# Attention feeding a rational feed-forward: value products of half a query range in one run, with the small column-tiled products and the weight conversion placed next to it

## The chip, the cores and the metric

The kernel runs on one core of one Trainium2 chip. The metric is the device time of that core in microseconds (us). Three executions of the kernel before took 981.39, 981.89 and 984.1 us; the median is 981.89. The execution that was profiled took 982.12 us, of which 980.3 us lie between its first and its last instruction.

## The reference, cut to what matters

The first stage is attention in which a query sees only the keys of its own hash bucket; the second is a feed-forward layer with a rational function between its two products.

```python
# attention: q, k, v are (4, 8, 768, 64); proj is (64, 6)
q_bits = (einsum('bhsd,dk->bhsk', q, proj) > 0)          # the same for k
mask = q_bucket[:, :, :, None] == k_bucket[:, :, None, :]
scores = where(mask, scale * q @ k.T, -1e9)
scores = scores - max(scores, axis=-1)
attn = exp(scores)
attn = attn / (sum(attn, axis=-1) + 1e-9)
x = attn @ v                                             # (3072, 512) once the heads are side by side
# feed-forward: w_in (512, 2048), w_out (2048, 512)
h = x @ w_in
P = a0 + a1*h + a2*h**2 + a3*h**3
Q = 1 + |b0|*|h| + |b1|*h**2
out = (P / (Q + 1e-6)) @ w_out
```

## The kernel before, in words

**Attention.** The 32 heads are worked in 16 pairs (p = 0 to 15), two heads (h) on the two halves of the 128 partitions. A pair has twelve steps: two halves of the queries (hf, 384 each) by six tiles of keys (kt). Step s = 6 hf + kt makes the scores of one key tile against 384 queries, for both heads, transposed (keys on the partitions). Operands are split in a high and a low float32r part (q1, k1 and q2, k2), and the bucket mask and the row maximum are carried as additional rows of q1 and k1, so that one product of 77 rows and one of 128 rows give masked and shifted scores (`scores`, lines 246 to 262). Each goes to a PSUM bank of 512 columns, tag "s", of which there are three, and ScalarE takes the exponential into an SBUF tile E, of which there are six. GpSimd adds the E of three successive steps into an accumulator acc.

**Value products.** `values` (lines 264 to 271) multiplies a tile of v (64 columns for each head) with E and adds up over the six key tiles of a half in a PSUM bank of its own, tag "v". These matmuls use 64 columns of the array, one head on each half, while scores use all 128. The operands are plain float32, and each matmul stands in the profile as two. `values_out` brings the half to SBUF on ScalarE (col, then xo), `values_store` stores it.

**Other column-tiled products.** `sums` (lines 283 to 292) adds up the accumulators over the keys with a column of ones, in strips of 32 array columns (psu), and ScalarE copies the outcome (sr). `bits` (lines 188 to 201) projects q and k of two pairs on the hash vectors, also in strips of 32 (psb), and VectorE turns the signs into mask rows mb at its end; `penalties` scales them on ScalarE, `maskrows` moves them by four DMAs into q1 and k1.

**Row maxima.** `maxstep` (lines 215 to 223) makes one tile of scores for a pair that comes later, into one of two double banks (ps_a, psm; psb takes turns with it in the same two), and VectorE reduces it to a column of m. When all twelve are done, `shift_turn` transposes m on the array (pst), VectorE clamps it (mt), and `shift_rows` moves it by a DMA into row 76 of q1 of that pair. Its scores can only begin after that DMA has landed.

**Operands.** `high` casts q and k of pair p on ScalarE, `low` subtracts the cast on VectorE, `high_move`, `second_low` and `second_high` move halves by DMAs, `load` and `load_v` fetch the next raw ones.

**Weights.** `weights(i)`, 32 times, loads a 512 KB piece of w_in or w_out (stored as 64-bit floats), turns it into float32 by two ScalarE and three VectorE instructions, and splits it in a high part (ScalarE) and a low one (VectorE). Pieces of w_out are stored to DRAM again (wo_d).

**What sets the order.** All engines keep the order of the program. The program is written by a table: `at(p, s, f)` enters f under the time 12 p + s, and lines 447 to 449 call all entries in the order of their times, entries of one time in the order in which they were made. So one unit of that table is a step, and an engine's queue holds its instructions in that order: a ScalarE or VectorE instruction that waits holds up all that stand behind it, and SP, which issues nearly all DMAs, does so too.

**Feed-forward.** After pair 15, `Ffn.step` runs 128 times: a product with w_in (`Gemm1`, psh, from line 458, which uses the banks "s" and "v"), the rational function on ScalarE and VectorE, a product with w_out (pso).

## Time and profile before

| | |
|---|---|
| median of three runs | 981.89 us (981.39 to 984.1) |
| the profiled execution: device time | 982.12 us |
| its span, first to last instruction | 980.3 us |
| first product of the feed-forward | 437.2 us |
| TensorE matmul busy | 957.6 us, 98% |
| VectorE busy | 835.4 us, 85% |
| ScalarE busy | 679.2 us, 69% |
| GpSimd busy | 436.8 us, 45% |

All times in rows are counted from the start of the span. PE is TensorE's matmul stream, PEld its weight loads, DVE VectorE, ACT ScalarE, POOL GpSimd, SP the engine that issues DMAs. All instructions carry line 61, that of the helper which issues them, so rows are told apart by the tiles' names, output before the arrow: pss are scores, psm the products for the maxima, psv values, psu sums, psb bits, pst the turned maxima. A row of the chain gives the start, the length and the piece of work, as "149.70 1.45 PE psv L61 x8": eight matmul instructions in the trace, which are two steps of value products.

### The profile page before, as it was taken

Reading aid. Unit: us, or ns where it says so; the run is one execution under the profiler, and the core shown is the slowest. Engines: PE = TensorE matmul, PEld = TensorE weight load, DVE = VectorE, ACT = ScalarE, POOL = GpSimd, SP = SyncE. Lnnn points to the kernel's source line nnn. Section 1 sums busy time; section 2 is a strip of 40 time slices with the busy share of each in tenths; the row PEclk is TensorE's granted clock in tenths of the full one; section 3 lists DMA queues with packets and bytes.
Section 4 is the critical chain, followed back from the end, with each engine's and each line's share of the span. In section 5 each row is a group of like instructions: output and inputs, shape, how many; then the busy total and the mean of one; then the engine's idle time right before and its main releaser. Section 6 shows DMA issues by size and latency. Waiting matters only on the chain.

```text
span 980.3 us, 14803 instructions
## 1 busy us (share of the span) xinstructions
PE 957.6 (98%) x5009; PEld 744.8 (76%) x5009; DVE 835.4 (85%) x1200; ACT 679.2 (69%) x1411; POOL 436.8 (45%) x396
## 2 busy tenths in 40 slices
PE   5899999999999999999999999999999999999998
PEld 2556666666656666559999999999999999999996
DVE  5487778777877777568999999999999999999996
ACT  2356767676666666678777777777777777777775
POOL 1257776777677777782222222222222222222222
PEclk7699999999999999999999999999999999999999
DMA  7656676767686767737502111011011021110000
GB/s 202 175 169 185 184 201 171 202 186 198 183 254 211 242 190 206 236 126 260 169 1 66 33 49 48 1 65 33 1 65 33 1 65 33 62 36 1 33 1 32
DMA packets 50491, 112.97 MB, mean 115 GB/s; under 512 B 9296, under 2 KB 21968, under 8 KB 50416
## 3 DMA queue, kind: packets, MB, share of 16 engines
q1 hardware_dynamic: 49580, 110.59, 37.9%
q10 hardware_dynamic: 836, 1.44, 0.6%
q8 instruction: 39, 0.64, 0.3%
q14 instruction: 36, 0.29, 0.1%
HBM read 56.82 MB, written 21.17 MB: 80 GB/s over the span
## 4 chain that ended last, share of the span: by engine, by line
PE 92%; DVE 3%; DMA 3%; ACT 1%; SPq 0%; issue 0%; ACTq 0%; DVEq 0%
PE psh L61 27%; PE pso L61 27%; PE pss L61 15%; PE psv L61 13%; PE psm L61 6%; PE psu L61 2%; DVE m L61 1%; PE psb L61 1%; DMA wr<-w_out 1%; DMA q<-lo 0%; SPq L61 0%; DVE c L61 0%; DMA v<-v 0%; DMA prj<-proj 0%; DMA q<-mt 0%
## 5 line engine op out<-in xcount | busy, mean ns | idle before, releaser
L61 POOL TENSOR_TENSOR gl<-c,gh 128x384 fp32r<-128x384 f32 x128 | 140.4, 1097 | 395.4 <-ACT gh L61 368.8
L61 DVE TENSOR_REDUCE m<-psm 128x1 f32<-128x768 f32 x192 | 182.0, 952 | 92.5 <-PE psm L61 90.4
L61 PE MATMUL pso<-wo,gh 128*128 128x512 f32 x768 | 241.1, 395 | 0.0
L61 ACT ACTIVATE E<-pss 128x384 f32<-128x384 f32 x384 | 168.3, 492 | 79.7 <-PE pss L61 72.8
L61 POOL TENSOR_TENSOR acc<-E,E 128x384 f32<-128x384 f32 x128 | 150.9, 1199 | 113.9 <-ACT E L61 113.9
L61 PE MATMUL pss<-q,k 77*128 77x384 f32 (+1 forms) x768 | 180.2, 357 | 2.5 <-DMA q<-mt 1.5
L61 PEld LDWEIGHTS pss<-q,k 77*128 77x128 f32 (+1 forms) x768 | 134.0, 192 | 60.3 <-issue 50.1
L61 PE MATMUL psh<-xl,wi_hi 128*128 128x384 f32 x512 | 172.1, 336 | 0.0
L61 PE MATMUL psh<-xh,wi_hi 128*128 128x384 f32 x512 | 171.8, 336 | 0.0
L61 PE MATMUL psh<-xh,wi_lo 128*128 128x384 f32 x512 | 171.6, 335 | 0.0
L61 PEld LDWEIGHTS pso<-wo,gh 128*128 128x128 f32 x768 | 142.9, 188 | 23.7
L61 PE MATMUL pso<-wo,gl 128*128 128x512 f32 x384 | 152.3, 397 | 0.3 <-POOL gl L61 0.3
L61 ACT ACTIVATE h<-psh 128x384 f32<-128x384 f32 x128 | 62.9, 492 | 123.9 <-PE psh L61 123.9
L61 PE MATMUL psv<-E,v 128*64 128x385 f32 x768 | 148.3, 503 | 0.0
L61 DVE SCALAR_TENSOR_TENSOR c<-c,ab,r 128x384 f32<-128x384 f32 x128 | 146.9, 1147 | 0.0
L61 POOL TENSOR_TENSOR acc<-acc,E 128x384 f32<-128x384 f32 x128 | 142.7, 1135 | 7.8 <-ACT E L61 5.9
L61 PE MATMUL psm<-k,q 76*128 76x384 f32 x384 | 107.8, 365 | 7.0 <-DMA k<-mb 3.7
L61 PEld LDWEIGHTS psh<-xh,wi_hi 128*128 128x128 f32 x512 | 96.1, 188 | 6.3 <-ACT w L61 0.6
L61 PEld LDWEIGHTS psh<-xl,wi_hi 128*128 128x128 f32 x512 | 96.1, 188 | 5.1
L61 PEld LDWEIGHTS psh<-xh,wi_lo 128*128 128x128 f32 x512 | 96.2, 188 | 0.0
L61 PEld LDWEIGHTS psv<-E,v 128*64 128x64 f32 x768 | 45.7, 136 | 60.0 <-issue 52.4
L61 ACT ACTIVATE c<-psh,ab 128x384 f32<-128x384 f32 x128 | 86.5, 676 | 1.7 <-POOL gl L61 1.7
(62 smaller groups left out, 1233.8 us busy)
## 6 DMA issues: line engine op xcount, KB each, us to landing
q<-q SPq DMA_DIRECT2D x48, 192.0 KB
k<-k SPq DMA_DIRECT2D x48, 192.0 KB
wr<-w_in SPq DMA_DIRECT2D x16, 512.0 KB
wr<-w_out SPq DMA_DIRECT2D x16, 512.0 KB
wo_d<-wr SPq DMA_DIRECT2D x16, 512.0 KB
wo<-wo_d SPq DMA_DIRECT2D x16, 512.0 KB
q<-lo SPq DMA_DIRECT2D x32, 192.0 KB
k<-lo SPq DMA_DIRECT2D x32, 192.0 KB
```

What stands on the lines that cost most here:

```text
L61: return self.tc.keep_in_program_order(issue(*args, **kwargs))
```

## The change

1. **Values in one run.** The twelve matmuls of `values` for a whole half (six steps by two heads) now all stand at one place of the table, 12 p + 6.3 for the first half and 12 p + 12.3 for the second: right after the first step of the half that follows. Before, pairs 1 to 14 did them two steps at a time, pairs 0 and 15 one step at a time.
2. **Tiles.** A half's six E stay alive until that run, so there are seven E instead of six; acc goes from six to five. The bank "v" becomes a fourth bank "s", and values take turns with scores, sums and the turned maxima.
3. **Beside the run.** `sums` goes from 14.5 to 12.31, directly behind the run of the second half. `bits` is split: its matmuls go to 0.32 of every second pair, directly behind `sums`; the VectorE part becomes `bucket_rows` at 0.5. `high` goes from 0 and 1 to 0.4, `low` from 2 and 3 to 0.45, `penalties` from 3 to 1.2, `maskrows` of every second pair from 4 to 2.
4. **Weights beside it.** The two ScalarE conversions of a piece stand at 5.4 of each half, the three VectorE instructions at 6.25 and 6.26, the high part at 6.9, the low part at 9.4.
5. **Shift rows.** `shift_turn` goes from 8 to 6.9, `shift_rows` from 10 to 8, `load` from 6 to 6.5.

```diff
-ACCS = 6
+ACCS = 5
-    E = [ep.tile([P, 2, HQ + 2], F32, name=f"E{i}") for i in range(6)]
+    E = [ep.tile([P, 2, HQ + 2], F32, name=f"E{i}") for i in range(7)]
...
+        PSB[p + which[0]] = ps
+
+    def bucket_rows(p, which=(0, 1)):
+        sl = slice(64 * which[0], 64 * which[-1] + 64)
+        ps, mb = PSB.pop(p + which[0]), MB[p + which[0]][0]
         nc.vector.tensor_scalar(out=mb[sl], in0=ps[sl, :, 0:HQ], ...)
...
-            ps = ps_b.tile([P, 512], F32, tag="s", bufs=3, name=f"pss{p}_{s}_{h}")
+            ps = ps_b.tile([P, 512], F32, tag="s", bufs=4, name=f"pss{p}_{s}_{h}")
-            AV[p, hf] = ps_b.tile([P, 512], F32, tag="v", name=f"psv{p}_{hf}")
+            AV[p, hf] = ps_b.tile([P, 512], F32, tag="s", bufs=4, name=f"psv{p}_{hf}")
...
-            if not 0 < p < NPAIR - 1:
-                at(p, s + 2.3, values, p, s)
-            elif s % 2:
-                at(p, s + 1.3, values, p, s - 1)
-                at(p, s + 1.3, values, p, s)
-            if s % NT == NT - 1:
-                at(p, s + (1.3 if 0 < p < NPAIR - 1 else 2.3), values_out, p, s // NT)
+        for hf in range(2):
+            for i in range(NT):
+                at(p, 6 * hf + 6.3, values, p, 6 * hf + i)
+            at(p, 6 * hf + 6.3, values_out, p, hf)
...
-            at(p, 14.5, sums, p)
+            at(p, 12.31, sums, p)
...
             for t in range(2):
-                at(p - 2, t, high, p, t)
-                at(p - 2, 2 + t, low, p, t)
-            if p % 2 == 0:
-                at(p - 2, 3 if p == 2 else 2, bits, p)
-                at(p - 2, 4 if p == 2 else 3, penalties, p)
+                at(p - 2, t if first else 0.4, high, p, t)
+                at(p - 2, 2 + t if first else 0.45, low, p, t)
...
-            at(p - 1, 8 + d, shift_turn, p)
-            at(p - 1, 10 if d == 0 else 9.6, shift_rows, p)
+            at(p - 1, 9.5 if p == 1 else 6.9, shift_turn, p)
+            at(p - 1, 9.6 if p == 1 else 8, shift_rows, p)
...
-        o = 6 * i - 3
-        late = (10.5, 12.5, 13.5, 14.5) if i < 2 * NFC - 1 else (10.5, 10.8, 11, 11.2)
-        spread(0, [o + x for x in (4, 7, 8, 9) + late], weights(i))
+        times = (1, 5.4, 6.25, 6.26, 6.9, 9.4, 11) if i < 2 * NFC - 2 else (1, 4, 5, 6, 6.5, 7.5, 8)
+        if i == 2 * NFC - 1:
+            times = (0.5, 3, 3.5, 4, 4.5, 5.5, 6.2)
+        spread(0, [6 * i + x for x in times], weights(i))
```

**TensorE, from the first step of pair 5 on.** The kernel before, after the last matmul of step 0; psv4_1 is the second half of pair 4, psu4 its sums:

```order
L61 MATMUL psm6_5_1686<-k1_6_1430,q1_6_1404 128x384 x2
L61 MATMUL psv4_1_1612<-E4_152,v_4_1238 64x385 x2
L61 MATMUL psv4_1_1612<-E5_153,v_4_1238 64x385 x2
L61 MATMUL pss5_1_0_1707<-q1_5_1135,k1_5_1161 128x384
...
L61 MATMUL psm6_7_1738<-k1_6_1430,q1_6_1404 128x384 x2
L61 MATMUL psv5_0_1746<-E0_148,v_5_1519 64x385 x2
L61 MATMUL psv5_0_1746<-E1_149,v_5_1519 64x385 x2
L61 MATMUL psu4_1751<-acc4_0_0_1423,ones_82 32x384 x2
```

And in the changed kernel:

```order
L61 MATMUL psm6_5_1668<-k1_6_1438,q1_6_1436 128x384 x2
L61 MATMUL psv4_1_1681<-E5_153,v_4_1235 64x385 x2
L61 MATMUL psv4_1_1681<-E6_154,v_4_1235 64x385 x2
L61 MATMUL psv4_1_1681<-E0_148,v_4_1235 64x385 x2
L61 MATMUL psv4_1_1681<-E1_149,v_4_1235 64x385 x2
L61 MATMUL psv4_1_1681<-E2_150,v_4_1235 64x385 x2
L61 MATMUL psv4_1_1681<-E3_151,v_4_1235 64x385 x2
L61 MATMUL psu4_1698<-acc4_0_0_1454,ones_82 32x384 x2
...
L61 MATMUL pss5_1_0_1726<-q1_5_1157,k1_5_1159 128x384
```

Four further value products were moved down to this place, and the sums, which stood behind step 2, now follow at once; steps 1 to 5 of pair 5 have no value products between them.

**ScalarE at the same place.** Before, from the last exponential of step 0; q1_7 and k1_7 are the casts of `high` for pair 7, sr4 the copy of the sums:

```order
L61 ACTIVATE E0_148<-pss5_0_1_1682 128x384
L61 CAST q1_7_1696<-qf7_1278 128x768
L61 COPY col4_1_1703<-psv4_1_1612 128x1
L61 ACTIVATE xo4_1_1704<-psv4_1_1612,col4_1_1703 128x384
L61 ACTIVATE E1_149<-pss5_1_0_1707 128x384
L61 ACTIVATE E1_149<-pss5_1_1_1711 128x384
L61 CAST k1_7_1722<-kf7_1280 128x768
L61 CAST wi_hi_128<-ws9_1589 128x512
L61 ACTIVATE E2_150<-pss5_2_0_1728 128x384
```

And in the changed kernel:

```order
L61 ACTIVATE E4_152<-pss5_0_1_1664 128x384
L61 COPY col4_1_1694<-psv4_1_1681 128x1
L61 ACTIVATE xo4_1_1695<-psv4_1_1681,col4_1_1694 128x384
L61 COPY sr4_1707<-psu4_1698 128x384
L61 CAST q1_7_1709<-qf7_1289 128x768
L61 CAST k1_7_1711<-kf7_1291 128x768
L61 CAST wi_hi_128<-ws9_1598 128x512
L61 ACTIVATE E5_153<-pss5_1_0_1726 128x384
L61 ACTIVATE E5_153<-pss5_1_1_1730 128x384
```

The cast q1_7, which stood ahead of everything that waits for the value products, now stands behind the copy of the sums, and both casts and the high part of a weight stand together ahead of the exponentials of step 1.

**VectorE at the same place.** In the changed kernel, from the maximum of step 0 of pair 5 (m6 from psm6_5) on; rz0, rd0 and rr0 belong to the reciprocals of the first batch, which stand here in three of the pairs:

```order
L61 TENSOR_REDUCE m6_1592<-psm6_5_1668 128x1
L61 TENSOR_SCALAR wr9_1597<-wr9_1597 128x512
L61 SCALAR_TENSOR_TENSOR ws9_1598<-ws9_1598,wr9_1597 128x512
L61 ISA ws9_1598<-wr9_1597,ws9_1598 128x1024
L61 TENSOR_TENSOR lo0_7_1713<-qf7_1289,q1_7_1709 128x768
L61 TENSOR_TENSOR lo1_7_1715<-kf7_1291,k1_7_1711 128x768
L61 TENSOR_SCALAR rz0_1717<-rs0_1579 128x48
...
L61 RECIPROCAL rr0_1719<-rd0_1718 128x48
L61 TENSOR_REDUCE m6_1592<-psm6_6_1737 128x1
L61 TENSOR_REDUCE m6_1592<-psm6_7_1755 128x1
L61 TENSOR_REDUCE m6_1592<-psm6_8_1770 128x1
L61 TENSOR_TENSOR wi_lo_129<-ws9_1598,wi_hi_128 128x512
```

Before, the same two subtractions stood one each between the maxima of steps 2, 3 and the next:

```order
L61 TENSOR_REDUCE m6_1583<-psm6_6_1718 128x1
L61 TENSOR_REDUCE m6_1583<-psm6_7_1738 128x1
L61 TENSOR_TENSOR lo0_7_1742<-qf7_1278,q1_7_1696 128x768
L61 TENSOR_REDUCE m6_1583<-psm6_8_1771 128x1
L61 TENSOR_TENSOR lo1_7_1779<-kf7_1280,k1_7_1722 128x768
L61 TENSOR_TENSOR wi_lo_129<-ws9_1589,wi_hi_128 128x512
```

They now stand together ahead of the maximum of step 1.

**SP within pair 4.** In the changed kernel, from the mask rows of pair 6 (mb6) to the shift row of pair 5 (mt5):

```order
L61 DMA q1_6_1436<-mb6_1426 12x768
L61 DMA k1_6_1438<-mb6_1426 13x768
L61 DMA x_d3_91<-xo3_1_1412 128x384
L61 DMA q2_5_1389<-q1_5_1157 64x768 x2
L61 DMA k2_5_1390<-k1_5_1159 64x768 x2
L61 DMA s_d0_104<-sr3_1424 2x384 x2
L61 DMA v_5_1520<-v 128x768
L61 DMA qf8_1570<-qT 128x768
L61 DMA kf8_1572<-kT 128x768
L61 DMA rs0_1579<-s_d0_104 128x48
L61 DMA wr9_1597<-w_in 128x1024
L61 DMA q1_5_1157<-mt5_None_1576 1x12x128
```

Before, the mask rows stood between v and the loads of q and k, and a store of xo between the weights and the shift row:

```order
L61 DMA v_5_1519<-v 128x768
L61 DMA q1_6_1404<-mb6_1452 12x768
L61 DMA k1_6_1430<-mb6_1452 13x768
...
L61 DMA qf8_1559<-qT 128x768
L61 DMA kf8_1561<-kT 128x768
L61 DMA wr9_1588<-w_in 128x1024
L61 DMA rs0_1592<-s_d0_104 128x48
L61 DMA x_d4_92<-xo4_0_1569 128x384
L61 DMA q1_5_1135<-mt5_None_1606 1x12x128
```

The mask rows moved ahead, so that in every second pair v, q, k and the weights are issued in one run directly ahead of the shift row.

More of the change, by code (lines that the diff above doesn't have):

```diff
@@ L283, in sums @@
     def sums(p):
-        ps = ps_b.tile([P, 512], F32, tag="s", bufs=3, name=f"psu{p}")
+        ps = ps_b.tile([P, 512], F32, tag="s", bufs=4, name=f"psu{p}")
         for k in range(PARTS):
@@ L421, in attention @@
     bits(0, (0,))
+    bucket_rows(0, (0,))
     penalties(0, (0,))
@@ L465, in __call__ @@
     def __call__(self, t, f):
-        tag, bufs = (("s", 3), ("v", 1), ("s", 3), ("s", 3))[f % 4]
-        ps = self.out[t, f] = self.pool.tile([P, 512], F32, tag=tag, name=f"psh{t}_{f}", bufs=bufs)[:, 0:NTK]
+        ps = self.out[t, f] = self.pool.tile([P, 512], F32, tag="s", name=f"psh{t}_{f}", bufs=4)[:, 0:NTK]
         fs = slice(f * P, f * P + P)
```

20 lines of the change are left out of this document (12 added, 8 removed).

## The prediction

> **What bounds the kernel now.** I read the page, then the busy time by stretches, then the chain of work that ended last inside one pair, and last the rows of the engines that the change moves. First the page, with PE's line and the chain by engine:
>
> ```profile
> span 980.3 us, 14803 instructions
> PE 957.6 (98%) x5009; PEld 744.8 (76%) x5009; DVE 835.4 (85%) x1200; ACT 679.2 (69%) x1411; POOL 436.8 (45%) x396
> PE 92%; DVE 3%; DMA 3%; ACT 1%; SPq 0%; issue 0%; ACTq 0%; DVEq 0%
> ```
>
> TensorE is the bound: 92% of the chain is its own work. The stretch of attention that I take is 88 to 414 us, thirteen pairs (columns: length, then busy us of PE, PEld, DVE, ACT and POOL, the clock granted, the DMA share, GB/s):
>
> ```profile
> 88.00:414.00 326.00, 323.05 (x1871) 205.49 (x1870) 244.66 (x315) 221.01 (x486) 239.40 (x209) 1.00 0.71 206
> ```
>
> TensorE has 3 us of idle time in 326, while VectorE, ScalarE and GpSimd are 25 to 32% idle. What the change can save there is TensorE's own time; what it can lose is waits that don't exist now. The feed-forward loses only a bank's name, and I cost it at nothing. Inside pair 4 the chain in order of time (start, length, piece) reads:
>
> ```profile
> 143.01 1.50 PE psb L61 x16
> ...
> 149.70 1.45 PE psv L61 x8
> 151.14 0.91 PE pss L61 x4
> 152.05 0.35 PE psm L61 x2
> 152.40 0.70 PE pss L61 x4
> ...
> 421.48 0.80 PE psv L61 x4
> ```
>
> Four score matmuls take 0.70 us, but 0.91 behind value products. The last row is of pair 15: one step of values takes 0.80, two take 1.45, so a step is 0.65 and each run costs 0.15 besides. A run of values thus costs 0.15 + 0.21 = 0.36 us beyond its products.
>
> **Part 1, fewer runs: -30 us.** In the order of the two programs TensorE goes from 128-column work to column-tiled work and back 122 times before and 39 times after (value runs 106 and 32; the others are bits and sums without values beside them). 83 x 0.36 = 30 us, all on the path that sets the end. The row is a direct measurement, so its error is small: 28 to 31. The Trainium skill, TensorEngine Tiling (Array Packing), Key Properties, says that a change of the tiling mode drains TensorE; TensorE: Matmul & The Clock Gate, Step-by-step, gives a drain as some 128 cycles, which at its 2.4 GHz is an estimated 0.05 us, so two drains a run would give 83 x 0.11 = 9 us. The rows show three times that, and I go by them.
>
> **Part 2, what now stands between a run and the next scores: +26 us.** What I need are durations of the instructions that gather at the end of a pair (last numbers: busy us, mean ns), and who waits for the sums:
>
> ```profile
> L61 ACT ACTIVATE E<-pss 128x384 f32<-128x384 f32 x384 | 168.3, 492 | 79.7 <-PE pss L61 72.8 <-POOL acc L61 2.3
> L61 ACT COPY sr<-psu 128x384 f32<-128x384 f32 x16 | 7.7, 479 | 35.1 <-PE psu L61 35.1
> L61 ACT CAST q<-qf 128x768 fp32r<-128x768 f32 x16 | 13.3, 832 | 2.3 <-DMA qf<-qT 2.3
> L61 ACT CAST k<-kf 128x768 fp32r<-128x768 f32 x16 | 13.4, 838 | 0.3 <-DMA kf<-kT 0.3
> L61 ACT CAST wi_hi<-ws 128x512 fp32r<-128x512 f32 x16 | 10.1, 630 | 0.0
> L61 DVE TENSOR_REDUCE m<-psm 128x1 f32<-128x768 f32 x192 | 182.0, 952 | 92.5 <-PE psm L61 90.4
> L61 DVE TENSOR_TENSOR lo<-qf,q 128x768 fp32r<-128x768 f32 x15 | 15.2, 1014 | 6.4 <-ACT q L61 4.3 <-DMA q<-lo 2.1
> L61 DVE TENSOR_TENSOR lo<-kf,k 128x768 fp32r<-128x768 f32 x15 | 14.2, 950 | 0.2 <-ACT k L61 0.2
> L61 DVE TENSOR_TENSOR wi_lo<-ws,wi_hi 128x512 fp32r<-128x512 f32 x16 | 16.6, 1039 | 0.0
> L61 DVE TENSOR_SCALAR mb<-psb,cst 128x768 fp32r<-128x768 f32 (+1 forms) x9 | 9.1, 1014 | 3.7 <-PE psb L61 3.7
> L61 ACT ACTIVATE mb<-mb,cst 128x768 fp32r<-128x768 f32 (+1 forms) x9 | 8.4, 936 | 7.5 <-DMA k<-mb 4.5 <-DVE mb L61 3.0
> ```
>
> ScalarE already waits for the sums (35.1 us). Before, that wait held up only exponentials; after, it also holds both casts, and the casts hold the exponentials of step 1 and, on VectorE, the two subtractions and all maxima behind them. Let T be the end of the sums.
>
> Pairs without bits. ScalarE: sr 0.48, q 0.83, k 0.84, wi_hi 0.63, so the first exponential ends at T + 2.8 + 0.5 = 3.3. TensorE does steps 1 and 2 in 0.91 + 0.35 + 0.70 + 0.35 = 2.3; four banks are then full, and step 3 waits 1.0 for the first to be read. VectorE: the subtractions start at T + 1.3, end at 3.3, the maximum of step 1 at 4.2; the psm of step 3, due at T + 2.3 + 0.7 = 3.0, needs that bank and waits until 4.2: 1.2 in all, the other wait included. Then VectorE has a maximum of 0.95 for each step of 1.05, and wi_lo (1.04) comes between: another 0.4. So 1.6.
>
> Pairs with bits. The bits cover 1.4 more, but their bank is one of the two of psm, and it is read by mb only behind the subtractions, at T + 3.3 + 1.0 = 4.3; the psm of step 2 is due at 1.4 + 0.9 + 0.35 + 0.7 = 3.4. 0.9 + 0.4 = 1.3.
>
> In three of the pairs without bits the reciprocals (rows of one such set in the chain) stand between subtractions and maxima:
>
> ```profile
> 161.63 0.91 DVE rz L61
> 162.54 0.11 DVE rd L61
> 162.67 0.92 DVE rd L61
> 163.60 0.22 DVE rd L61
> ```
>
> That is 2.2 us. There are 13 such places (p = 3 to 15): 7 x 1.6 + 6 x 1.3 + 3 x 2.2 = 25.6, taken as 26. Bounds: 10, if VectorE and ScalarE issue back to back with 0.1 less for each instruction, as E does (168.3 / 384 = 0.44, not 0.49); 36, if the weights wait as well.
>
> **Part 3, the shift row comes late: +22 us.** SP's issues in pair 4 (start, length), and two transfers from the chain, issue to landing:
>
> ```profile
> 144.20 1.29 SPq L61 DMA_DIRECT2D q<-q  x2
> ...
> 148.01 1.10 SPq L61 DMA_DIRECT2D s_d<-sr  x2
> 149.21 0.33 SPq L61 DMA_DIRECT2D v<-v  x1
> 149.75 0.79 SPq L61 DMA_DIRECT2D q<-mb  x1
> ...
> 155.56 0.42 SPq L61 DMA_DIRECT2D wr<-w_in  x1
> ...
> 157.37 0.78 SPq L61 DMA_DIRECT2D q<-mt_None  x1
> ...
> 280.88 3.13 DMA wo_d<-wr
> 284.03 5.21 DMA wr<-w_out
> ```
>
> Before, the shift row (q<-mt) is issued 1.8 us behind the weights, and step 10 to step 12 take two steps of 2.1 us; after, it is behind them directly, and a step without values is only 0.70 + 0.35 = 1.05. In pairs with bits: mb on VectorE ends at T + 4.3, its scaling on ScalarE (0.94, penalties) at 5.3; SP stands before the mask rows until then. Four issues of mask rows 3.1, xo some 0.5, four halves (q<-q and k<-k, 0.65 each) 2.6, sums 1.1, v 0.33, q and k as the weights, 0.42 each: the weights are issued at T + 13.8 and land 5.2 later, at 19.0, the shift row, last in that queue, not before. Scores of the next pair are due at T + 1.4 (bits) + 11 x 1.05 + 0.4 + 4.1 (run) + 1.3 = 18.8. So next to nothing at best. But v, q, k (128 x 768 floats each) and the weights (512 KB), 1.7 MB, now go out in 2 us where the mask rows stood between; at 206 GB/s for 0.71 of the DMA share, 290 GB/s at most, they alone take 5.8 us, and the halves ahead (four of 64 x 768), 0.8 MB, 2.7 more. From v's issue at T + 12.6 that is a landing between 18.4 and 21.1 even without the 2 us or so that a transfer needs beside its bytes. I take a wait of 1.8 at 12 pairs, 22 us; the ends are 0 and 36 (3.0 each).
>
> **Part 4, pair 15: +3 us.** It has no psm, so a step is 0.70 on TensorE and 2 x 0.44 on ScalarE; five steps in a row twice, 10 x 0.18, and the run of 4.1 us after the last score has nothing beside it, where three steps stood before. 2 to 5.
>
> **Sum.** -30 + 26 + 22 + 3 = +21 on 982.12, the profiled execution's own time (0.2 above the median): 1003 us. Three edits I cost at nothing. The VectorE part of a weight, three instructions each shorter than wi_lo's 1.04, stands beside a run of 6 x 0.65 + 0.15 = 4.05, so it is covered; without that it would cost up to 3.1 a half. The two conversions on ScalarE stand there too, ahead of exponentials that TensorE needs only after the run. GpSimd's eight additions a half take 239.40 / 26 = 9.2 us; they start with the exponential of step 1, 1.5 after a run, and end at 10.7; the last product of the sums is due at 6 x 1.05 + 0.2 + 4.05 + 1.0 = 11.6. Five acc and seven E suffice then; a GpSimd that is 1 us slower would cost 1 us a pair, and that is within the range.
>
> **The rivals.**
>
> *Faster: the gain stays.* The engines issue more closely than the means say, and the shift row lands in time. Part 2 goes to 10 and part 3 to 0 to 5: 982 - 30 + 10 + 3 = 965 to 970. It decides at one place: the maximum of step 1 must end before psm of step 3 is due, T + 3.0. For it speaks that a dense exponential costs 0.44; against it that the casts can't start before sr, which waits for the last matmul. Chance 0.15.
>
> *No change.* Part 2 as worked out, part 3 near 0: 982 - 30 + 26 + 3 = 981. This takes a DMA queue that drains as fast as before; the denser issue speaks against. 0.06.
>
> *Slower still: the DMAs of the second weights hold ScalarE.* The chain at 280.88 shows a store (3.13) and a load behind it (5.21) that ended late and held the conversions, and with them the scores. After, a load stands 4.4 steps ahead of its conversion, 4.6 us. If that misses by 2 us in each of the 16 pieces of w_out, 32 more: 1035. The run of values (4.1) mostly covers it: 0.10.
>
> *The clock falls.* In the start-up the granted clock is 0.50 while TensorE is busy for two thirds:
>
> ```profile
> 20.00:30.00 10.00, 6.78 (x18) 4.42 (x18) 5.84 (x9) 1.42 (x3) 1.81 (x1) 0.50 0.75 164
> ```
>
> Should waits of 2 to 3 us bring that back, a fall as long as this row costs 5 us of work; four of them give 1023. TensorE: Matmul & The Clock Gate, What's actually happening, in the Trainium skill, says that such a gate follows recent activity. The stretch of attention stays at over 85% busy by my sum: 0.03.
>
> *The edit doesn't do what it says.* The order shows the twelve matmuls in one run, so this is out but for the cost of a run: should an entry cost a run of twelve as much as six small ones, part 1 is nothing and the time is 1033. 0.02, counted with the slower two.
>
> **How the numbers follow.** Forecast 0.64 (985 to 1028: parts 2 and 3 with one of them near an end), faster 0.15, no change 0.06, the slower ones 0.15. The range takes in "no change" and leaves out the faster rival and the far end of the slower ones: 980 to 1030. About 0.3% (3 us) is what a measurement of this kernel can tell from none. Faster by more than that 0.15, within 0.06, slower 0.79.
>
> **What would show it.** Right: 32 runs of 24 psv instructions, each 4.05 us, with four score matmuls behind them still at 0.91; PE waiting for DVE m (psm) and ACT E (pss) at the third step after psu, 1 to 1.6 us and more where the reciprocals are; DMA q<-mt ahead of the first pss of most pairs. Wrong: PE's idle time in attention still near 3 us, or pairs shorter than 24 us without bits, or a psm that never waits.

## The result, and the profile after

The changed kernel takes 1050.94 us (median of four runs, 1047.56 to 1052.1), the kernel before 982.78 (four runs, 981.39 to 984.1): the ratio is 1.067, with a 95% interval from 1.064 to 1.070. The profiled execution took 1051.55 us. The forecast had the sign and lay 48 us too low; the range ended at 1030.

The page of the changed kernel, with its span, the engines' busy time, the granted clock in 40 slices and the chain by engine, answers to the first rows shown of before:

```profile
span 1049.8 us, 14789 instructions
PE 978.2 (93%) x5009; PEld 772.8 (74%) x5009; DVE 852.8 (81%) x1200; ACT 675.6 (64%) x1411; POOL 409.0 (39%) x397
PEclk8689998899988899699999999999999999999999
PE 79%; DVE 8%; DMA 7%; issue 2%; ACT 2%; SPq 1%; POOL 1%; DVEq 0%; ACTq 0%
```

TensorE executes the same 5009 instructions, but they take 978 us and not 958, and 21% of the chain is now something else than TensorE's work, DMA and VectorE above all, where it was 8%. The row of the clock gives the granted clock in tenths. It shows 8, and twice 6, again and again in its first twenty slices, which are the start-up and attention; in the feed-forward it is 9, and the mean from 506.6 us on is 1.00. The same thirteen pairs as before (88 to 414 us there) now lie between 91 and 476.5 us:

```profile
91.00:476.50 385.50, 340.16 (x1868) 227.09 (x1867) 262.27 (x317) 216.42 (x484) 209.89 (x206) 0.91 0.60 174
```

They take 385.5 us, not 326. TensorE is idle for 45 us of them instead of 3, and its mean clock is 0.91 instead of 1.00. The feed-forward is the same: from its first product, at 506.6 us, to the end of the span are 543.2 us, and 543.1 before.

The chain in order of time (start, length, piece), from the run and the sums at the start of pair 4 to the third step of pair 5, shows both losses:

```profile
147.35 4.03 PE psv L61 x24
151.38 1.52 PE psu L61 x16
...
153.30 0.84 ACT q L61
...
155.04 0.95 DVE lo L61
155.99 0.94 DVE mb L61
...
156.98 0.62 PE psm L61 x2
...
169.33 5.63 DMA q<-mt_None
...
177.35 5.66 PE psv L61 x24
...
187.63 0.91 DVE rz L61
...
190.99 0.82 DVE m L61
...
191.86 1.01 PE psm L61 x2
```

A run of twelve value products takes 4.03 us. Behind the sums come the cast on ScalarE, the subtraction on VectorE and only then mb, which reads the bank of the bits; the next psm needs that bank and waits for it. The shift row (q<-mt) is issued at 169.33 and lands 5.63 later, and the scores of pair 5 wait for it. And then the same run of 24 instructions takes 5.66 us, with nothing to wait for: TensorE runs at half clock in its first 3.3 us. Behind that run the reciprocals (rz) stand ahead of the maximum, and psm takes longer as well (1.01 against 0.62).

The waits of the same stretch (engine and line, what it waited for, us in total, times, longest):

```profile
DVE lo L61 <- ACT q L61: 54.6, 12, 6.1
...
PE pss L61 <- DMA q<-mt_None: 23.1, 9, 4.2
PEld psm L61 <- DVE m L61: 18.3, 20, 3.7
...
PE psm L61 <- DVE m L61: 12.0, 10, 3.4
```

Scores wait nine times for the shift row, products for maxima up to twenty times for VectorE (the row of the weight load and that of the matmul partly show the same waits), and VectorE's subtractions twelve times for the cast on ScalarE.

**Where the 69 us are.** I took the start of each TensorE instruction to the start of the next, from the first score of pair 1 to the first product of the feed-forward. An instruction has an ordinary distance at full clock (0.175 us for a score or a maximum, and so on, with the price of entering and leaving a run). What is above it inside a stretch at half clock counts as slow work, up to twice the ordinary distance, and what is above 0.3 us beyond that counts as a wait.

| us | ordinary work | waits | slow work | small rests | sum | at half clock |
|---|---|---|---|---|---|---|
| before | 365.8 | 3.8 | 0 | 4.1 | 373.7 | 0 |
| after | 345.1 | 57.0 | 37.0 | 7.6 | 446.6 | 81.9 |

The sum grows by 72.9; 3.5 of them come back because pair 1 starts at 60.0 instead of 63.5. So the runs save 21 us of TensorE's work, the waits cost 53 and the clock costs 37. Four rows show how the clock goes, each 3.41 us long (length, busy us of PE, PEld, DVE, ACT and POOL, clock, DMA share, GB/s):

```profile
67.97:71.38 3.41, 1.89 (x11) 1.57 (x10) 3.41 (x5) 2.64 (x7) 1.93 (x2) 1.00 0.70 155
71.38:74.79 3.41, 3.41 (x13) 3.40 (x12) 2.53 (x4) 1.97 (x4) 2.93 (x4) 0.50 0.95 247
...
170.37:173.78 3.41, 1.48 (x9) 1.16 (x7) 3.08 (x4) 1.57 (x4) 3.41 (x4) 1.00 0.91 306
173.78:177.20 3.42, 2.11 (x6) 1.78 (x6) 0.00 (x0) 2.13 (x4) 2.34 (x3) 0.50 1.06 292
```

In the first of each two rows TensorE waits and the clock is still full; in the next it is 0.50. A busy row of this length has 13 matmul instructions at half clock (the second row) where some 20 fit at full clock; the fourth row still holds a part of the wait. There are 13 such falls in the attention part, 3.4, 6.8 or 10.2 us long.

### The profile page after: what moved, and what is told of

Same layout as the page of the kernel before. It is cut to its first block, busy times and chain, and to the rows that moved or that the text cites. A ratio compares the mean times of both kernels' runs of the same rounds, so it can differ in the third digit from the quotient of the medians.

```text
span 1049.8 us, 14789 instructions
## 1 busy us (share of the span) xinstructions
PE 978.2 (93%) x5009; PEld 772.8 (74%) x5009; DVE 852.8 (81%) x1200; ACT 675.6 (64%) x1411; POOL 409.0 (39%) x397
## 4 chain that ended last, share of the span: by engine, by line
PE 79%; DVE 8%; DMA 7%; issue 2%; ACT 2%; SPq 1%; POOL 1%; DVEq 0%; ACTq 0%
PE psh L61 26%; PE pso L61 25%; PE psv L61 13%; PE pss L61 7%; PE psm L61 5%; DMA q<-mt_None 4%; DVE m L61 3%; PE psu L61 2%; DVE lo L61 1%; ACT q L61 1%; SPq L61 1%; DVE rd L61 1%; DVE mb L61 1%; POOL acc L61 1%; ACT E L61 1%
## 5 line engine op out<-in xcount | busy, mean ns | idle before, releaser
L61 DVE TENSOR_REDUCE m<-psm 128x1 f32<-128x768 f32 x192 | 177.2, 950 | 67.9 <-PE psm L61 64.3
L61 POOL TENSOR_TENSOR acc<-E,E 128x384 f32<-128x384 f32 x128 | 133.6, 1063 | 214.0 <-ACT E L61 214.0
L61 PE MATMUL pss<-q,k 77*128 77x384 f32 (+1 forms) x768 | 184.6, 368 | 30.8 <-DMA q<-mt_None 23.7
L61 ACT ACTIVATE E<-pss 128x384 f32<-128x384 f32 x384 | 162.5, 495 | 51.6 <-PE pss L61 44.2
L61 PEld LDWEIGHTS pss<-q,k 77*128 77x128 f32 (+1 forms) x768 | 145.2, 205 | 48.8 <-issue 25.6
L61 PEld LDWEIGHTS pso<-wo,gh 128*128 128x128 f32 x768 | 142.9, 188 | 23.7
L61 POOL TENSOR_TENSOR acc<-acc,E 128x384 f32<-128x384 f32 x128 | 134.3, 1069 | 4.3 <-ACT E L61 4.3
L61 PE MATMUL psm<-k,q 76*128 76x384 f32 x384 | 114.6, 385 | 22.6 <-DVE m L61 15.8
L61 PEld LDWEIGHTS psv<-E,v 128*64 128x64 f32 x768 | 57.8, 153 | 82.7 <-issue 73.8
L61 PEld LDWEIGHTS psm<-k,q 76*128 76x128 f32 x384 | 76.3, 214 | 38.6 <-DVE m L61 25.4
```

What stands on the lines that cost most here:

```text
L61: return self.tc.keep_in_program_order(issue(*args, **kwargs))
```

## The experiments

Theory W: the waits come first (casts and reciprocals ahead of the maxima, the shift row behind bulk loads), and a wait of about 1.7 us or more makes the clock fall. Rival R: the clock falls for the long runs, and would do so without the waits. All runs have the columns of the table above; the intervals are of the ratio to the kernel before.

| run | median us | ratio, 95% | ordinary work | waits | slow work | at half clock |
|---|---|---|---|---|---|---|
| late shift row in the kernel before | 1001.0 | 1.011 to 1.022 | 365.8 | 13.6 | 8.6 | 20.5 |
| ladder of waits in the kernel before | 1029.8 | 1.044 to 1.050 | 370.0 | 30.8 | 15.0 | 34.1 |
| kernel before, runs only | 1020.4 | 1.032 to 1.041 | 348.0 | 40.1 | 14.4 | 30.7 |
| after, shift row on another queue | 1047.3 | 1.056 to 1.068 | 345.1 | 55.1 | 34.0 | 75.1 |
| after, waits filled | 1043.8 | 1.054 to 1.065 | 378.5 | 36.6 | 17.3 | 37.5 |
| after, reciprocals beside a run | 1032.7 | 1.042 to 1.055 | 345.1 | 51.1 | 23.6 | 51.2 |
| after, shift row ahead of loads | 1018.5 | 1.031 to 1.038 | 345.1 | 37.0 | 21.9 | 54.6 |
| after, casts ahead of the run | 1008.9 | 1.019 to 1.030 | 345.1 | 35.1 | 19.1 | 44.4 |
| the same, shift row on another queue | 1010.2 | 1.021 to 1.031 | 345.1 | 34.7 | 21.3 | 47.8 |
| casts, and shift row ahead of loads | 1009.1 | 1.021 to 1.030 | 345.1 | 29.4 | 18.4 | 44.4 |
| these, and reciprocals, subtractions, stores | 990.1 | 1.003 to 1.009 | 345.1 | 21.5 | 8.3 | 20.5 |
| these, and even loads later | 979.3 | 0.993 to 0.997 | 345.1 | 14.5 | 6.3 | 13.7 |

### Is it the waits or the runs? The kernel before with waits, and no run

First a late shift row, in the kernel before:

```diff
-            at(p - 1, 10 if d == 0 else 9.6, shift_rows, p)
+            at(p - 1, 11.9 if d == 0 else 9.6, shift_rows, p)
```

> The kernel before with one edit: the shift row of pairs 2 to 15 is entered at 11.9 instead of 10, so that TensorE waits for it at the start of most pairs; no run of values is longer than before. Theory W: about 2 us of wait at a dozen pairs, 20 us, and falls of the clock behind the longer ones, 5 to 15 us more: 1005 to 1020 us, half clock inside attention. Rival R: waits alone, 995 to 1003 us, and a full clock from 44 us to the end as in the kernel before.

Measured: 1001.0 us, below the 1005 to 1020 of W and within the 995 to 1003 of R, so the time alone doesn't decide; the clock does, since R expected none of what follows. There are four falls, each behind a wait for the row (3.0, 3.0, 0.9 and 0.7 close together, and 3.2 us); single waits of 0.9 to 1.0 us have none behind them. The first, in two neighbouring rows:

```profile
162.79:166.20 3.41, 1.03 (x6) 0.70 (x5) 3.34 (x6) 0.87 (x2) 2.56 (x3) 1.00 0.04 8
166.20:169.61 3.41, 2.77 (x8) 2.07 (x10) 1.69 (x3) 1.55 (x3) 0.00 (x0) 0.50 0.83 217
```

TensorE is busy for 1.03 us of the first and has half its clock in the second, in a kernel that has no run longer than two steps. So R's condition isn't needed.

Then the disputed thing by itself: the kernel before, with one wait of a set length in each of the pairs 2 to 13.

```diff
+    def pause(p, k):
+        ps = ps_b.tile([P, 512], F32, tag="s", bufs=3, name=f"psg{p}")
+        nc.tensor.matmul(ps[:, 0:HQ], K2[p][:, 0, 0:P], Q2[p][:, 0, 0:HQ], start=True, stop=True)
+        g = sm.tile([P, HQ], F32R, tag="g", name=f"g{p}")
+        nc.scalar.copy(g, ps[:, 0:HQ])
+        for _ in range(k - 1):
+            nc.scalar.copy(g, g.bitcast(F32))
+        ps = ps_b.tile([P, 512], F32, tag="s", bufs=3, name=f"psf{p}")
+        nc.tensor.matmul(ps[:, 0:HQ], g[:, 0:P], g, start=True, stop=True)
...
+    for p, k in zip(range(2, 14), (1, 2, 3, 4, 5, 6, 8, 2, 3, 4, 5, 3)):
+        at(p, 4.35, pause, p, k)
```

> The kernel before, without any of the change, with one wait of TensorE added in each of the pairs 2 to 13: a matmul of its own, 1, 2, 3, 4, 5, 6, 8, 2, 3, 4, 5 and 3 copies of 128x384 on ScalarE behind it, and a matmul that waits for the last copy; nobody reads the result. By the copies' length the waits are about 0.7, 1.3, 1.8, 2.3, 2.8, 3.3, 4.4, 1.3, 1.8, 2.3, 2.8 and 1.8 us, 26 us in all, one in each 27 us. Theory W: no fall behind the waits of up to 1.3 us, a fall of 3.4 us or a multiple of it within 4 us behind most of those from 1.8 us on; the half clock is 30 to 70 us long in all and costs 12 to 30 us: 983 + 32 + 20 = 1035, between 1022 and 1048. Rival R (the clock hangs on long runs and not on waits): 983 + 26 + 6 = 1015 at most, at full clock.

Measured: 1029.8 us, of which 15 us are slow work: the added waits (27 us) and matmuls would give about 1015 at full clock. The falls start at 157.0, 187.8, 218.5, 245.8, 279.9, 392.6 and 423.3 us, and any two of these differ by a whole multiple of 3.413 us (30.7 is 9 of them, 27.3 is 8, 112.7 is 33). That holds within each of the profiled runs; the offset differs from run to run. So I cut the attention part on that grid. Rows of five of the waits, 1.38, 1.93, 1.93, 2.47 and 3.01 us long in this order:

```profile
126.32:129.73 3.41, 2.30 (x12) 1.30 (x9) 2.92 (x4) 1.91 (x5) 2.58 (x2) 1.00 0.64 191
129.73:133.15 3.42, 3.42 (x20) 2.21 (x19) 2.83 (x4) 1.95 (x6) 2.30 (x2) 1.00 0.55 158
...
153.63:157.04 3.41, 1.75 (x9) 0.75 (x6) 2.94 (x4) 2.88 (x6) 2.58 (x2) 1.00 0.50 149
157.04:160.45 3.41, 3.41 (x13) 3.27 (x11) 1.51 (x2) 1.64 (x4) 1.83 (x2) 0.50 0.74 240
...
331.12:334.53 3.41, 3.07 (x17) 1.60 (x15) 3.18 (x4) 3.41 (x8) 1.67 (x2) 1.00 0.63 172
334.53:337.95 3.42, 2.10 (x12) 2.10 (x13) 1.82 (x4) 2.23 (x6) 1.49 (x2) 1.00 0.25 65
337.95:341.36 3.41, 3.41 (x20) 2.20 (x19) 2.69 (x5) 2.13 (x7) 1.94 (x3) 1.00 0.97 326
...
358.43:361.84 3.41, 2.19 (x12) 0.73 (x10) 3.41 (x5) 2.85 (x7) 3.13 (x2) 1.00 0.75 205
361.84:365.25 3.41, 2.43 (x13) 2.24 (x13) 1.28 (x4) 2.25 (x6) 0.94 (x2) 1.00 0.46 154
...
389.15:392.56 3.41, 0.76 (x4) 0.76 (x5) 1.50 (x3) 2.47 (x5) 1.15 (x1) 1.00 0.48 159
392.56:395.97 3.41, 3.41 (x13) 2.97 (x13) 2.04 (x3) 1.96 (x4) 1.83 (x2) 0.50 0.48 172
```

The same wait of 1.93 us brings a fall where it lies in one cell of the grid (153.63, busy 1.75) and none where a border cuts it (334.53, busy 3.07 and 2.10); even 2.47 us, cut in two, brings none. All twelve:

| wait, us | TensorE busy in the cells that hold it, us of 3.41 | fall behind it |
|---|---|---|
| 0.84, 1.38, 1.38 | 3.34 and 2.92; 2.30; 3.05 and 2.67 | none |
| 1.93, 2.47 (cut by a border) | 3.07 and 2.10; 2.19 and 2.43 | none |
| 1.93, 1.93 | 1.75; 1.75 | 3.4; 6.8 us |
| 2.46, 3.01 | 2.88 and 1.76; 2.19 and 1.90 | 3.4; 3.4 us |
| 3.01, 3.38, 4.64 | 3.33 and 0.76; 0.59; 2.23 and 0.23 | 6.8; 6.8; 3.4 us |

So W holds, in a sharper form: what counts is not the wait's length but TensorE's busy time in a cell of 3.41 us. In the attention parts of all fourteen profiled kernels there are 1499 cells at full clock. In 78 of them TensorE was busy for up to 1.97 us, and the clock was at half in the cell behind 75; of 23 with 1.97 to 2.16 us behind 15; of the 1398 with more behind none. The kernel before has no cell under 2.48 us. Among the 1398 are 130 that value products filled for 3.0 us or more, all in kernels with long runs, and full clock followed each of them: no run brought a fall by itself.

The Trainium skill, TensorE: Matmul & The Clock Gate, What's actually happening, says that the gate watches a free-running window of 3413 ns, and gives the half clock to the time after an idle window. The grid agrees with the first (3.413 us); the second is too mild here, since a window that is busy for 1.90 us of 3.41 was enough, and the measurement decides.

### The long runs with their waits filled

The changed kernel with score products that nobody reads, 7 to 24 ahead of the scores that wait and 18 ahead of a maximum at the reciprocals:

```diff
+    def busy(p, n):
+        ps = ps_b.tile([P, 512], F32, tag="s", bufs=4, name=f"psf{p}_{n}")
+        for _ in range(n):
+            nc.tensor.matmul(ps[:, 0:HQ], K2[p][:, 0, 0:P], Q2[p][:, 0, 0:HQ], start=True, stop=True)
...
+    for p, n in ((3, 12), (4, 7), (5, 18), (7, 16), (8, 10), (9, 14), (11, 24), (12, 14), (13, 22)):
+        at(p - 1, 11.95, busy, p - 1, n)
+    for p in (5, 9, 13):
+        at(p, 2.9, busy, p, 18)
```

> The changed kernel with extra score products whose result nobody reads, placed on TensorE just ahead of the scores that wait longest (7 to 24 of them, about 0.17 us each, before pairs 3, 4, 5, 7, 8, 9, 11, 12 and 13, and 18 of them ahead of the maximum at the reciprocals in pairs 5, 9 and 13). The result keeps its values; about 30 us of work is added to TensorE where it waits. Theory W: the engine has no wait long enough to lose its clock at these places, so the half clock (82 us in the attention part) falls to under 25 us, which gives back 25 to 35 us, and the added work costs only what exceeds the waits, up to 10 us: 1015 to 1035, faster than the changed kernel although it does more. If the clock doesn't depend on the waits: the added work gives nothing back, 1051 to 1070, with the half clock still near 80 us.

Measured: 1043.8 us, above the 1015 to 1035 expected, and its interval just meets that of the changed kernel. What the table shows is clearer than the total: 33.4 us more work on TensorE, 20.4 less waits and 19.7 less slow work, at half clock for 37.5 us instead of 81.9, with the same long runs. That speaks against R. My size was off: the fillers covered 20 us of waits and not 25 to 30, and the delay that they brought made five new ones of 1.8 to 2.1 us (scores of pairs 10 and 14, and three products for maxima, which waited for a mask row's DMA), four of them with a fall behind.

### The waits one by one

**Casts ahead of the run.** In the changed kernel:

```diff
-                at(p - 2, t if first else 0.4, high, p, t)
+                at(p - 2, t if first else 0.1, high, p, t)
```

> The changed kernel with one edit: the casts of pairs 3 to 15 stand at 0.1 instead of 0.4, so on ScalarE ahead of everything that waits for the run of values and for the sums. Theory W: the waits for maxima and banks behind the sums (25 us) go, and with them the three falls of the clock behind the reciprocals (31 us at half clock): 1051 - 25 - 15 = 1011 us; the waits for the shift row stay or grow, since TensorE arrives earlier. Rival R: 1026 us, clock 0.95. Rival D (only the shift row counts, TensorE waits there for what it gained before): 1040 or more.

Measured: 1008.9 us, 42 less than the changed kernel: 22 less waits and 18 less slow work. ScalarE now casts beside the run instead of behind sr, and waits of psm fall from 21.2 to 5.6 us. The shift row stays, as the profile says of 80 to 450 us:

```profile
PE pss L61 <- DMA q<-mt_None: 22.1, 8, 4.7
```

**Reciprocals beside a run.** In the changed kernel:

```diff
-            spread(p, (19, 24.5, 25.5), recips(p // NHP))
+            spread(p, (19, 30.4, 33), recips(p // NHP))
```

> The changed kernel with one change: VectorE's reciprocals (three times in the program, 2.2 us each) stand beside the next run of values, not at the end of a pair between the subtractions and the maxima. Theory W (waits first, then a slow clock for a multiple of 3.4 us): the three waits of 3.4 us go (10 us), and with them the three falls of 10.2 us behind them (31 us at half clock, of 82 that cost 37 us in all, so about 14 us): 1051 - 10 - 14 = 1027, between 1020 and 1033. If the clock doesn't hang on these waits: 1051 - 10 = 1041, with the half clock still near 80 us.

Measured: 1032.7 us, with 51.2 us at half clock. The three waits of 3.4 us are gone, and so are the falls behind them. The time is within W's 1020 to 1033, and the 1041 that the waits alone would give lies above the interval (its end, 1.0547 times the 983.45 of the kernel before beside it, is 1037.3).

**Shift row on another queue.** In the changed kernel, the shift row's DMA from ScalarE's queue:

```diff
-            move(nc, Q1[p][76:77, :, :].rearrange("o h (i c) -> o (h i) c", c=P), src)
+            move(nc, Q1[p][76:77, :, :].rearrange("o h (i c) -> o (h i) c", c=P), src, nc.scalar)
```

> The changed kernel with one edit: the shift row of pairs 1 to 15 is issued by ScalarE instead of SP, so it stands behind no other transfer of its queue. In the trace of the changed kernel TensorE waits 24 us in all for that transfer, and eight falls of the granted clock (37.6 us at half clock) begin 1 to 4 us behind those waits. Theory W (waits cost their length, and a wait of about 1.7 us or more makes the clock fall): both go, 1051 - 24 - 18 = 1009 us, falls left only behind the waits at the reciprocals, mean clock about 0.97. Rival R (the long runs of column-tiled float32 matmuls lower the clock by themselves): only the waits go, 1027 us, clock still 0.95. Rival L (the lag of VectorE and ScalarE behind the sums is all that counts, the shift row is absorbed by it): 1045 or more.

Measured: 1047.3 us. That is a time of rival L (1045 or more), but the edit didn't remove the wait (20.3 us in twelve pairs, 23.7 in ten before this edit), so the run tests none of the three. In its chain the row of pair 5 is issued at 170.27 and lands no earlier:

```profile
170.27 5.59 DMA q<-mt_None
```

That is the time that it took from SP's queue (5.63). Over the pairs of attention that have the row in their chain it took 3.2 to 6.2 us from SP's queue and 4.0 to 5.8 from ScalarE's. ScalarE's conversion of the weights that SP had issued ahead of the row waits for their landing and starts at 175.67; the row lands at 175.86. So it waits for what the DMA engines still have to move, whatever queue it comes from. The Trainium skill, Trainium Kernel Development and Optimization, Key Constraints, says that DMAs of all issuing engines share the same 16 DMA engines and interleave, and that more issuing engines save only issue time; this agrees.

Together with the casts:

> Both edits. Theory W: waits and falls of the clock nearly all go, what is left is the gain of fewer runs, 982 - 30 + 10 = 962 to 970 us, faster than the kernel before, clock 0.98 as there. Rival R: the runs are all there, so the clock still falls: 1000 us or more, clock 0.95 to 0.96.

Measured: 1010.2 us, as with the casts alone (1008.9). The 962 to 970 of W rested on a row that lands early, and it did not: scores wait 13.3 us for it instead of 22.7, and products for maxima wait 9.3 us for VectorE instead of 4.5. The time is one that R expected (1000 or more), but with these waits left it doesn't tell the two apart.

**Shift row ahead of the loads.** In the changed kernel, on SP's queue alone:

```diff
-            at(p - 1, 9.6 if p == 1 else 8, shift_rows, p)
+            at(p - 1, 9.6 if p == 1 else 7.1, shift_rows, p)
...
-            at(p - 4, 6.5, load, p)
+            at(p - 4, 7.2, load, p)
...
+        if i % 2 and i < 2 * NFC - 2:
+            times = (1.3, *times[1:])
```

> The changed kernel with one change on SP's queue alone: the shift row is issued ahead of the load of a later pair's q and k and ahead of the odd weights' load, so that no bulk transfer stands before it. Casts and bits stay beside the run as in the changed kernel. Theory W (waits first, and each wait of about 1.7 us or more halves TensorE's clock for 3.4 us or a multiple): the waits of pss for the shift row (about 24 us) go, and with them about half of the 37 us that the half clock costs: 1051 - 24 - 18 = 1009, between 1000 and 1018; the falls that are left follow waits of psm, above all those for the reciprocals (pairs 6, 10, 14). Rival R (the clock falls for the long runs, whatever the waits): 24 us less alone, 1027, and the half clock still about 75 to 82 us long. If the shift row still lands late: over 1040.

Measured: 1018.5 us. The waits of pss fall from 31.0 to 7.9 us, and of these 0.6 are for the row; 15 us of slow work go with them. The total is just above the 1000 to 1018 that W expected; the waits at the reciprocals grew, from 3.4 us each to between 3.9 and 4.9.

**The runs alone.** The kernel before, with the values in runs of a half, seven E, five acc and four banks "s", and nothing else moved (cut to the lines that move the values):

```diff
...
+        for hf in range(2):
+            for i in range(NT):
+                at(p, 6 * hf + 6.3, values, p, 6 * hf + i)
+            at(p, 6 * hf + 6.3, values_out, p, hf)
...
```

> The kernel before with the runs of twelve steps' values alone (seven tiles of exponentials, five of sums, four banks for all); sums, bits, casts, weights, shift row and loads keep the places that they have in the kernel before. It is the price of the run by itself. Theory W: 30 us less work on TensorE; the shift row keeps its earlier place, so no wait for it; behind the runs a lag of VectorE and ScalarE of 10 to 20 us is left, in waits that are mostly under 1.5 us, so the clock mostly stays: 968 to 985. Rival R (long runs lower the clock or bring the cost with them): over 1000, with the half clock in the attention part over 40 us long.

Measured: 1020.4 us, so W's 968 to 985 was wrong, and the time is where R put it (over 1000). The clock is not what R expected (30.7 us at half clock, under its 40); the surprise is the waits, 34.7 us for maxima. The chain in pair 4, ahead of the run of its first half:

```profile
155.70 0.07 DVE m L61
...
157.44 1.51 DVE wi_lo L61
158.96 0.88 DVE m L61
...
159.88 0.99 PE psm L61 x2
```

With the values gone from between them, the steps ahead of a run follow each other in 1.05 us, about what a maximum takes (0.95), and the subtractions of operands and weights (lo, wi_lo) still stand among these maxima. Twelve pairs wait 1.5 us there, and three 3.5 to 4.5 us at the reciprocals. So runs cost waits unless the other engines' work is moved beside them; the change moves most of it, but puts the casts behind the sums.

### A version without long waits

Casts ahead of the run and the shift row ahead of the loads, together:

> The changed kernel with the casts of q and k ahead of the run (as in the run before of that alone, 1009 us) and the shift row ahead of the bulk loads. Theory W: from 1009 the 23 us of waits for the shift row go, and the 19 us of half clock that followed them: 962 to 975, faster than the kernel before (983), the granted clock about 0.98 as before. Rival R: about 1009 - 23 = 986 or more, and the half clock in the attention part still over 30 us long.

Measured: 1009.1 us, no better than the casts alone, and where R put it (986 or more, over 30 us at half clock). The waits for the shift row are gone, but in the three pairs with reciprocals waits of 3.0, 3.7 and 4.9 us are left (the first for a mask row's DMA, which stands on SP's queue behind the store of the reciprocals), with falls of 10.2, 13.7 and 13.7 us behind them. Then, besides, the reciprocals beside a run, the subtractions just ahead of a maximum that had stood in front, the loads of q and k behind those of the weights and the stores of the second weights earlier:

```diff
-                at(p - 2, 2 + t if first else 0.45, low, p, t)
+                at(p - 2, 2 + t if first else 0.35, low, p, t)
...
-            at(p - 4, 7.2, load, p)
+            at(p - 4, 7.35, load, p)
...
-            spread(p, (19, 24.5, 25.5), recips(p // NHP))
+            spread(p, (19, 30.4, 33), recips(p // NHP))
...
-        times = (1, 5.4, 6.25, 6.26, 6.9, 9.4, 11) if ...
+        times = (1, 5.4, 6.25, 6.26, 6.9, 9.4, 9.9) if ...
```

> The changed kernel with the casts ahead of the run and the shift row ahead of the bulk loads, as in the run before (1009 us), and besides: reciprocals beside a run, the subtractions of pair 3 ahead of its predecessor's maxima, the load of a later pair's q and k behind that of the weights, and the stores of the second weights earlier. No wait of TensorE over about 1.5 us is left by the order. Theory W: the 19 us of waits for maxima fall to under 8, no fall of the clock is left or one or two (18 us of slow work to under 4): 960 to 978, faster than the kernel before (983) although it has the same long runs. If long runs bring slow work by themselves: 985 or more, with over 25 us of half clock in the attention part.

Measured: 990.1 us, above the 960 to 978 expected; 20.5 us at half clock are left, under the over 25 of the other expectation. Four waits of 1.9 to 3.5 us are left. The chain shows a new cause at the first:

```profile
162.61 7.17 DMA k<-lo
...
169.97 1.78 DVE lo L61
171.76 0.88 DVE m L61
...
172.68 0.61 PE psm L61 x2
```

The subtraction writes the one buffer of lo that there is for k, which the DMA of the pair before still reads; that DMA lands 7.17 us after its issue, behind loads of weights, q and k. So the loads of even pairs go behind it:

```diff
-            at(p - 4, 7.35, load, p)
+            at(p - 4, 7.35 if p % 2 else 16.5, load, p)
```

> The run before (990 us: casts ahead of the run, shift row ahead of bulk loads, reciprocals beside a run) with one more change on SP's queue: the loads of q and k for even pairs stand 9 steps later, behind the transfers that free the tiles which the next subtractions write. In that run the subtractions of k waited up to 2.7 us for those transfers, four waits of TensorE for maxima (1.9 to 3.5 us, 11 us in all) stood behind them, and two falls of the clock of 10.2 us (8 us of slow work). Theory W: waits for maxima from 15 us to 4 to 8, no fall or one left: 990 - 8 - 7 = 975, between 968 and 982, at or below the kernel before (983). If something else than the waits makes the clock fall: above 984, with about 20 us of half clock still in the attention part.

Measured: 979.3 us, at 0.995 of the kernel before (0.993 to 0.997); the execution that was profiled, and that the table shows, is the slowest of twelve, 983.4. Its stretch from 90 to 414 us:

```profile
90.00:414.00 324.00, 317.75 (x1904) 217.51 (x1904) 272.84 (x320) 221.57 (x493) 222.60 (x211) 0.98 0.75 210
```

It executes 1904 matmuls in 324 us, where the kernel before did 1871 in 326. One fall of 10.2 us, behind a wait of 2.2, and one of 3.4 in pair 15 are left in the stretch from pair 2 on. The kernel has the same runs as the changed kernel and is faster than the one before, by 0.5% (some 4 us), so the runs' gain is real, if small in the total, and the changed kernel lost it to waits and to the clock behind them.

**What ends a fall.** Here the traces say more than W. The fall behind the wait at the reciprocals of pair 5, in the changed kernel, has three cells, and the next is at full clock:

```profile
190.84:194.25 3.41, 2.39 (x7) 2.39 (x8) 3.17 (x5) 0.50 (x2) 0.51 (x2) 0.50 0.55 112
194.25:197.67 3.42, 3.42 (x12) 3.42 (x12) 2.09 (x3) 2.54 (x6) 3.42 (x4) 0.50 0.91 252
197.67:201.08 3.41, 3.41 (x11) 1.45 (x12) 2.28 (x5) 0.90 (x3) 0.41 (x1) 0.50 0.64 175
201.08:204.49 3.41, 3.41 (x23) 1.65 (x20) 0.71 (x2) 0.49 (x2) 0.00 (x0) 1.00 0.53 155
```

TensorE is busy throughout the second and the third. The second holds scores and products for maxima alone, and the half clock stays; the third holds 2.52 us of value products, and it ends. Over all fourteen profiles there are 163 cells at half clock. The 35 in which TensorE was busy for less than 3.37 us were all followed by another. Of the 128 others, full clock followed all 83 with 1.3 us of value products or more, and only 4 of the 41 with less than 1.1 us (3 of the 4 between). So value products go with the end of falls and not with their start, and R has it the wrong way round. But values in runs leave stretches of steps without value products between them, and a fall that begins there mostly lasts until the next run: all 21 falls of over 6.8 us are in kernels with long runs, and of the 11 in the kernel before with waits none is longer. That part of the clock's price does come with the change; no run here measures it by itself, nor shows why scores don't bring the clock back.

## Why the prediction was wrong

The forecast put four terms in a sum; their totals came out within 7 us of their sizes, in part by luck. The step that failed is the one that left the clock out of it.

**The bound and the gain.** TensorE bounds the kernel, and a run takes 4.03 us (4.05 forecast). Part 1, -30, came out as -21 in the stretch of the table. Some 2.6 of the rest is work of pair 0, four steps of values at 0.65, which now falls into the stretch, so about -23 is what compares. The price of 0.36 a run held; the count was wrong. In the traces TensorE enters column-tiled work (values, sums, bits) 107 times before and 34 times after, and in this stretch 96 and 31 times: 65 x 0.36 = 23.4. The forecast's 122 and 39 come out, to within one, only when the turned maxima (pst) are counted as well, and one of these among scores cost some 0.1 us before, not 0.36.

**Part 2, +26.** Waits of psm are 21.2 and those for a bank at the third step 5.2 (six of 0.87): 26.4. The total is as forecast, its parts are not. A pair without bits waits 0.87 for a bank of scores (1.6 forecast, mostly for psm), one with bits 1.07 + 0.42 = 1.5 for psm (1.3 forecast), the reciprocals 3.4 each on top of the 0.87 (2.2 forecast), and 2.1 us at 68.7 and 91.4 us stand in no term. That these cancel is luck. Casting ahead of the run took most of it away, which confirms the chain from sums to cast to subtraction to maximum.

**Part 3, +22.** The waits for the shift row add up to 24.1 us, in nine pairs of 1.2 to 4.2 and not in twelve of 1.8. The forecast's bulk transfers were the cause: with the row ahead of them the waits went.

**Part 4, +3.** Pair 15 and the sums ahead of it show waits of 5.2 us, 2 more than forecast. Of the edits costed at nothing, GpSimd's additions were free: sums wait 1.7 us for GpSimd in all, and only at pair 14. For the two that concern the weights no run tests it.

**The step that failed: the rival "The clock falls".** It had the mechanism, from the start-up row of 0.50, and a time of 1023 by four falls of 5 us; it got 0.03, because "the stretch of attention stays at over 85% busy by my sum". The mean of a stretch says nothing on that: TensorE was busy for 340 us of the 385.5 of the thirteen pairs, which is 88%, and the clock fell all the same. The runs showed that a cell of 3.41 us decides, and the forecast's own waits, 1.8 us at the shift rows and 3.5 at the reciprocals, were long enough to empty one to under 2 us. There were 13 falls, 82 us at half clock, and they cost 37 us, 2.8 each. Without them the four terms as measured give -21 + 26 + 24 + 5 = 34, that is 1016, inside the range; with the clock's 37 it is 71, near the 69 us seen (the kernel before has 3.8 us of waits of its own, which come off; the small rests and the earlier start of pair 1 cancel).

**The other rivals.** "Faster" failed where it said that it would, at the third step: it waits for its psm in pairs with bits and at the reciprocals, and for its bank of scores in the others. The DMAs of the second weights held ScalarE for 10.8 us in all, but the chain through pairs 1 to 15 has no DMA of these weights in it. Every part of the edit did what it says.

## What to carry to other kernels

Where TensorE is the bound, price a wait not only by its length: ask what it leaves of TensorE's busy time in a few microseconds, since a fall behind such waits cost 2.8 us of slow work on average here, on top of the wait. A run that saves an engine's work pays only when all that the other engines do for the next step stands beside it or ahead of it, and when no small, urgent transfer stands behind bulk loads. Move these first, and the run last.

## What the hardware showed that was not expected

- The clock halves on a grid of 3.413 us that is fixed within a run: behind a cell with up to 1.97 us of busy TensorE in 75 of 78 cases, behind more than 2.16 us never (of 1398).
- It comes back only behind a half-clock cell in which TensorE was busy throughout, and there it hangs on the kind of work: behind 1.3 us or more of value products (64-column, float32) in 83 of 83 cells, behind less than 1.1 us, the rest scores and maxima (128-column, float32r), in 4 of 41. Why is open.
- A DMA of 6 KB from a second issuing engine took as long as from the first (5.59 and 5.63 us, in pair 5) behind the same bulk loads.
